# The last V tile in one load, w3 in two loads of two rows per partition, and w3's products by halves, in a one-token attention-and-MLP decode kernel

## The chip, the cores and the metric

The kernel runs on one core of a Trainium2 chip, as one launch. The metric is device time in microseconds (us), from three timed runs of which the median counts. Lower is better. A core has five engines with an instruction queue each: TensorE (PE for products, PEld for the loading of their stationary operand), VectorE (DVE), ScalarE (ACT), GpSimd (POOL) and SyncE (SP), which here only issues transfers. All transfers between memory outside the core and on-chip memory are carried out by 16 DMA engines.

## The reference, cut to what matters

Eight sequences, one new token each (B = 8), model width D = 512. Attention has 32 query heads over 8 key-value heads of width 128 and sees the last 2048 positions of the caches. Then follows an MLP block with two layer norms one after the other; its first part multiplies by w1 and w2 only token-shifted values, which are zero for a single token, so that only w3 (512 x 1792) and w4 (1792 x 512) remain.

```python
def _A_ref(x, k_cache, v_cache, wq, wo):
    ...
    k = jnp.repeat(k_cache[:, :, Sk - W:, :], rep, axis=1)
    v = jnp.repeat(v_cache[:, :, Sk - W:, :], rep, axis=1)
    scores = jnp.einsum("bhqd,bhkd->bhqk", q, k) * (Dh ** -0.5)
    p = _softmax(scores, axis=-1)
    o = jnp.einsum("bhqk,bhkd->bhqd", p, v)
    return (lambda x, *d: x.transpose(*d))(o, 0, 2, 1, 3).reshape(B, Sq, Hq * Dh) @ wo
...
    h2 = _gelu(_layernorm(x1, axis=-1) @ w3) @ w4
    return x1 + h2

x = A_x
h = x + _A_ref(_layernorm(x, axis=-1), A_k_cache, A_v_cache, A_wq, A_wo)
h2 = h + _B_ref(_layernorm(h, axis=-1), B_w1, B_w2, B_w3, B_w4)
```

All inputs and the output are bf16. Some 79 MB are read: 32 MB of K, 32 MB of V, 4 MB each of wq and wo, 1.75 MB each of w3 and w4 (MB of 2^20 bytes).

## The kernel before, in words

The caches come in 16 units n = 0 to 15: a unit is one sequence b = n // 2 and four of its heads. `load_k(n)` (L469) and `load_v(n)` (L475) fetch one unit of K or V as 128 partitions of 16,384 bytes, 2 MB in all, into rings of four buffers, `knat` and `vnat`. V of load 15 is the exception: four loads of 512 KB, 4096 bytes per partition, each with a semaphore of its own (`sem_vl`, L194). SP issues every load of the kernel in one written order, all through the function at L202, one after the other: the K and V units, two loads of wo of 1 MB on the way, then V of load 15, four loads of wo of 512 KB, w3, w4. A load waits on SP for the products that used its buffer last.

Each engine's work is listed by hand in program order (`Engine.op`, L60), with the semaphores that it waits for; each engine runs its list in that order. TensorE's work on a unit is four transposes of K (L308), two groups of scores (L323), and later, with the softmax done, the products of the probabilities with V (`pe_PV`, L406), in four quarters w = 0 to 3 of a unit. For the last three units each quarter is 16 products of 128x128 with 16 columns (`f_last`, L410, L414), whose result DVE scales (L448) and TensorE turns (`turn_o`, L454, L460) and DVE copies to `o2` (L465).

The end of the kernel is this list on TensorE: quarters of V 13 and 14; quarter 0 of V 15, the turn of unit 14, quarters 1 to 3 of V 15; `pe_wo` for the first four groups of wo (L498 to L503; 4 small products that add x at L496, then 64 at L501); the turn of unit 15; `pe_wo` for the last four groups (64 at L501). The result is h transposed: h's 512 columns lie as four column blocks nb of 128 x 8 in `hT_ps`. Then come the two layer norms: column sums by a product with a constant matrix (L627, L648), small DVE steps (L624 to L631, L651 to L654) and two ACT steps (L649, L650). `hb` (L628) is h minus its mean, in bf16, and is what the products with w3 take; the norm's factor comes in later, at L661.

w3 is loaded in four loads of 128 rows of w3 each, 3584 bytes per partition, which share one semaphore (L606, L607). The products with w3 (`pe_w3`, L641) are 14 output blocks f with four products each, one for each block kc of 128 rows: 28 for the first half of the blocks, into one PSUM bank, then 28 for the second half, into another. The stationary operand takes every fourth column of w3, every second for the last two blocks (`w3_cols`, L636). The first of them waits for `hb` and for all four loads. After each half DVE multiplies (L661) and ACT applies GELU (L663). Then TensorE adds the residual (L667) and runs the products with w4 (L676), four at a time in four column strips of the array, in parts that wait for GELU's two halves and for w4's loads: 28 products with w4's first two loads, 4, 16 with the third (`sem_w4b`), 8 with the fourth (`sem_w4c`). DVE and ACT copy the result (L685, L687), and SP stores it (L690).

Of the kernel before, what the change touches and what calls it, by code (L numbers as in the profile page):

```python
# [11 lines left out]
B = 8  # L12
# [10 lines left out]
FC = F // 128  # L23
KC = D // 128
# [6 lines left out]
U = 4  # L31
RR = 32
NCU = W // RR
UL = NCU * DH

NK = 4
NV = 4
# [44 lines left out]
def bass_sequential_preLN__sliding_block_cached__mixer_s_mlp__decode_kernel(  # L82
# [19 lines left out]
    NUN = NB * NU  # L102
# [4 lines left out]
    with es:  # L107
        sb = lambda shape, dtype, name: es.enter_context(nc.sbuf_tensor(name, shape, dtype))
        ps_t = lambda shape, dtype, name: es.enter_context(nc.psum_tensor(name, shape, dtype))
        S = lambda name: es.enter_context(nc.semaphore(name))  # L110

        knat = sb([128, NK, UL], dt.bfloat16, "knat")
        vnat = sb([128, NV, UL], dt.bfloat16, "vnat")
        wbig = sb([128, KC * H * DH], dt.bfloat16, "wbig")
        wq_v = wbig[:, :].rearrange("p (k n) -> p k n", k=KC)
        wo_v = wbig[:, :].rearrange("p (g k n) -> p g k n", g=G, k=R)
        w3_sb = knat[:, 0, 0:KC * F].rearrange("p (k f) -> p k f", k=KC)
        w4_sb = knat[:, 1, 0:FC * D].rearrange("p (c n) -> p c n", c=FC)
# [13 lines left out]
        x_sb = sb([B, D], dt.bfloat16, "x_sb")  # L132
# [33 lines left out]
        at = [0]  # L166

        def tl(n, bf=False):
            t = tail[:, at[0]:at[0] + n]
            at[0] += n  # L170
            return t.bitcast(dt.bfloat16) if bf else t
# [4 lines left out]
        hb = tl(NH // 2, True)  # L176
# [3 lines left out]
        out_sb = sb([B, D], dt.bfloat16, "out_sb")  # L180
# [10 lines left out]

        sem_k = [S(f"sem_k{i}") for i in range(NK)]
        sem_v = [S(f"sem_v{i}") for i in range(NV)]
        sem_vl = [S(f"sem_vl{i}") for i in range(U)]  # L194
        sem_wl = [S(f"sem_wl{i}") for i in range(2)]
        sem_x, sem_wq, sem_wo, sem_w3, sem_w4a, sem_w4b, sem_w4c, sem_out = (
            S(n) for n in ("sem_x", "sem_wq", "sem_wo", "sem_w3", "sem_w4a", "sem_w4b", "sem_w4c", "sem_out"))
        PE, AC, DV, PO, SP = (Engine(S(n)) for n in ("s_pe", "s_act", "s_dve", "s_pool", "s_sp"))

        def dma(eng, dst, src, sem, *waits):  # L200
            def f(e):
                e.dma_start(dst, src).then_inc(sem, 16)  # L202
            eng.op(f, *waits, inc=False)
# [16 lines left out]
        e = DV.op(lambda e: e.bn_stats(st6[:, :], x_sb[:, :]), X)  # L220
        e = DV.op(lambda e: e.bn_aggr(mv[:, :], st6[:, :]), e)
        e = AC.op(lambda e: e.activation(rstd[:, :], mv[:, 1:2], ACT.Sqrt, bias=eps1[0:B, :], scale=1.0), e, e_eps)
        e = DV.op(lambda e: e.reciprocal(rstd[:, :], rstd[:, :]), e)
# [30 lines left out]
        e = PE.op(pe_xT, e_xln, e_idb)  # L254
# [12 lines left out]
        e = DV.op(lambda e: e.tensor_scalar(q_d, S_ps[0][:, 0:H * B], inv_sqrt_dh, None, ALU.mult), e_q)  # L267
# [17 lines left out]
        e_T, e_Tlo, e_Thi, e_lo, e_hi, e_QK, e_PV = {}, [], [], [], [], {}, {}  # L285
# [111 lines left out]
            e_rL[b] = DV.op(lambda e: e.tensor_tensor(rLk[:, s, :, :], r_bc, k_bc, ALU.mult), e_r, e_mK)  # L397

        def V(n, w):
            if n == NUN - 1:  # L400
                return sem_vl[w], 16
            return sem_v[n % NV], 16 * (n // NV + 1)

        e_ev_o, e_fold = {}, {}
# [70 lines left out]
        def load_v(n):  # L475
            b, t = divmod(n, NU)
            src = A_v_cache[b, J * t:J * (t + 1), W0:SK, :].rearrange("j (r c) d -> r j (c d)", r=RR)
            if n < NUN - 1:
                dma(SP, vnat[:, n % NV, :], src, sem_v[n % NV], e_PV.get(U * (n - NV + 1) - 1))
                return  # L480
            for w in range(U):
                cs = slice(w * UL // U, (w + 1) * UL // U)
                dma(SP, vnat[:, n % NV, cs], src[:, :, cs], sem_vl[w], e_PV.get(U * (n - NV + 1) - 1))

        def load_wo(m, sem, g=2):
            dma(SP, wo_v[:, m:m + g, :, :].rearrange("p g k n -> p g (k n)"),
                A_wo[m * R * DH:(m + g) * R * DH, :].rearrange("(g p k) n -> p g (k n)", p=128, k=R), sem, e_q)

        hT_ps = S_ps[0]
        e_wo = []  # L490

        def pe_wo(groups, *waits):
            def f(e):
                if groups[0] == 0:
                    for nb in range(KC):
                        e.matmul(hT_ps[:, nb * B:(nb + 1) * B], x_sb[:, nb * 128:(nb + 1) * 128],  # L496
                                 ident_b[0:B, 0:B], start=(nb == 0), stop=False, skip_group_check=True)
                for g in groups:  # L498
                    for k in range(R):
                        for nb in range(KC):  # L500
                            ins = e.matmul(hT_ps[:, nb * B:(nb + 1) * B], wo_v[:, g, k, nb * 128:(nb + 1) * 128],  # L501
                                           o2[:, g, k, :], start=False, stop=(g == G - 1 and k == R - 1),
                                           skip_group_check=True)  # L503
                return ins
            e_wo.append(PE.op(f, e_exp[NB - 2], X, *waits))
# [32 lines left out]
        for n in range(NUN):  # L538
# [4 lines left out]
            if n >= LVD:  # L543
                load_v(n - LVD)
            if n in WO_AT:
                load_wo(WO_G[WO_AT.index(n)], sem_wo)
            i = U * n
# [35 lines left out]
        for n in range(NUN - LVD, NUN):  # L583
            load_v(n)
# [15 lines left out]
        for a in range(2):  # L600
            for g in (WO_L + 2 * a, WO_L + 2 * a + 1):
                load_wo(g, sem_wl[a], 1)
            pe_wo((WO_L + 2 * a, WO_L + 2 * a + 1), e_scale[NUN - 1], (sem_wl[a], 32))
        e_gl = AC.op(lambda e: e.activation(scratch[:, 1:2], scratch[:, 0:1], ACT.Sqrt), e_warm)

        for k in range(KC):  # L606
            dma(SP, w3_sb[:, k, :], B_w3[128 * k:128 * (k + 1), :], sem_w3, e_T[U * (NUN - NK + 1) - 1])  # L607
        FA = 12
        w4_a = B_w4[0:FA * 128, :].rearrange("(a p c) n -> p a (c n)", p=128, c=4)
        for a, sem in ((0, sem_w4a), (1, sem_w4a), (2, sem_w4b)):  # L610
# [10 lines left out]
        def bc(a, k=KC):  # L621
            return bass.AP(tensor=a.tensor, offset=a.offset, ap=[a.ap[0], [0, k], [1, B]])
# [5 lines left out]
        e_hb = DV.op(lambda e: e.tensor_tensor(v3(hb[:, :]), v3(hs[:, :]), bc(st1), ALU.add), e_mu, e_hs)  # L628
        e = DV.op(lambda e: e.tensor_tensor(v3(hc[:, :]), v3(hs[:, :]), bc(st1), ALU.add))
        e = DV.op(lambda e: e.tensor_tensor(hsq[:, :], hc[:, :], hc[:, :], ALU.mult), e)  # L630
# [3 lines left out]
        FH = FC // 2  # L634

        def w3_cols(kc, f):  # L636
            a, c = divmod(f, 4)
            s = 4 if a < 3 else 2
            return w3_sb[:, kc, 512 * a + c:512 * a + c + 127 * s + 1:s]

        def pe_w3(e, n, f0, f1):  # L641
            for f in range(f0, f1):
                for kc in range(KC):
                    ins = e.matmul(y_ps[n][:, f * B:(f + 1) * B], w3_cols(kc, n * FH + f),
                                   hb[:, kc * B:(kc + 1) * B], start=(kc == 0), stop=(kc == KC - 1))
            return ins

        e = PE.op(lambda e: e.matmul(st2, ones_v[:, :], vsum[:, :], start=True, stop=True), e_vs, e_sc[NUN - 1])  # L648
# [3 lines left out]
        e_r1 = DV.op(lambda e: e.reciprocal(rr[:, B:2 * B], vv[:, B:2 * B]), e1)  # L652
        e = DV.op(lambda e: e.tensor_tensor(v3(xb[:, :]), v3(hc[:, :]), bc(rr[:, B:2 * B]), ALU.mult), e_r1)
        e_fin = DV.op(lambda e: e.tensor_tensor(p32(fin[:, :]), v3(hs[:, :]), v3(xb[:, :]), ALU.add), e, e_pad)  # L654
        e_y = [PE.op(lambda e: pe_w3(e, 0, 0, FH), e_hb, (sem_w3, 16 * KC), e_lo[-1], e_hi[-1], e_lo[-2], e_hi[-2]),
               PE.op(lambda e: pe_w3(e, 1, 0, FH))]
        e_gT = []
        for n in range(2):
            cs = slice(n * FH * B, (n + 1) * FH * B)
            gs = slice(n * FH * 32, (n + 1) * FH * 32)  # L660
            e = DV.op(lambda e, n=n, cs=cs: e.tensor_tensor(v3(g_x[:, cs]), v3(y_ps[n][:, 0:FH * B]),  # L661
                                                            bc(rr[:, 0:B], FH), ALU.mult), e_y[n], e_rr)
# [3 lines left out]
        z_ps = S_ps[1][:, 0:128]  # L666
        PE.op(lambda e: e.matmul(z_ps, fin[:, :], ident_f[:, :], start=True, stop=False, skip_group_check=True),  # L667
              e_fin, e_exp[NB - 1])
        for lo, hi, waits in ((0, FH, (e_gT[0], (sem_w4a, 32))),
                              (FH, 8, (e_gT[1],)),  # L670
                              (8, FA, ((sem_w4b, 16),)),
                              (FA, FC, ((sem_w4c, 16),))):
            def pe_w4(e, lo=lo, hi=hi):
                for fc in range(lo, hi):
                    for nb in range(KC):
                        ins = e.matmul(z_ps[32 * nb:32 * (nb + 1), :], gT[:, fc * 32:(fc + 1) * 32],  # L676
                                       w4_sb[:, fc, nb * 128:(nb + 1) * 128], start=False, stop=(fc == FC - 1),
                                       tile_position=(0, 32 * nb), skip_group_check=True)
                return ins
            e_z = PE.op(pe_w4, *waits)  # L680
        e_out = []
        for nb in range(KC):
            o, z = out_sb[:, nb * 128:(nb + 1) * 128], z_ps[32 * nb:32 * nb + B, :]
            if nb % 2:
                e_out.append(AC.op(lambda e, o=o, z=z: e.activation(o, z, ACT.Copy), e_z))  # L685
            else:
                e_out.append(DV.op(lambda e, o=o, z=z: e.tensor_copy(o, z), e_z))  # L687
# [39 lines left out]
```

## Time and profile before

| What | Value |
|---|---|
| timed runs, median (lowest to highest) | 195.89 us (195.77 to 195.93) |
| the profiled execution's own time | 195.99 us |
| its span, first to last instruction | 194.7 us |
| mean granted TensorE clock | 0.893 of full speed; 0.50 from 170 us to the end |
| PE / PEld / DVE / ACT / POOL busy | 75% / 59% / 51% / 46% / 4% of the span |
| DMA engines busy in slices 2 to 38 of 40 | 90% or more in each |
| read from memory | 79.18 MB, 407 GB/s over the span |
| DMA packets | 7506 |

All times inside the kernel are us from the start of the span. About 1.3 us of the profiled time lie outside the span. A DMA packet is one contiguous run that one DMA engine moves: a load of 128 partitions gives each of the 16 engines 8 of them, and 4-byte ones for the semaphore. A load has landed when the last of the 16 engines is through; the semaphore events in the trace tell when each of them was.

### The profile page before, as it was taken

The page shows a single profiled execution, that of the slowest core. Times are in us where ns is not written, and L with a number is a line of the kernel's source. Part 1 is how long each engine was busy: PE and PEld are TensorE (multiplying, and loading weights), DVE is VectorE, ACT ScalarE, POOL GpSimd, SP SyncE. Part 2 cuts the span into 40 slices and gives each one's busy share as a digit, 9 for nine tenths or more (in the row PEclk, how much of TensorE's full clock was granted, in tenths as well). Part 3 has the DMA queues.
Part 4 walks back from the last instruction along what each step waited for, and adds up shares of the span by engine and source line. Part 5 has one row for each costly group of instructions (what it writes and reads, how often), then busy time and mean ns, then how long its engine had stood idle before and what let it go on. Part 6 is the DMA issues. An engine that isn't in the chain of part 4 may idle for free.

```text
span 194.7 us, 4474 instructions
## 1 busy us (share of the span) xinstructions
PE 146.1 (75%) x1972; PEld 115.0 (59%) x1972; DVE 100.1 (51%) x256; ACT 89.6 (46%) x115; POOL 7.7 (4%) x29
## 2 busy tenths in 40 slices
PE   0028985978999794969498868988497897879765
PEld 0027862765768564746495738765485674768653
DVE  5402445785667582738165664468154975731131
ACT  6000566764848453745153824564264754250041
POOL 5001101001000100010001000010000000000000
PEclk9999999999999999999759997999889999655555
DMA  6999999999999999999999999999999999999981
GB/s 224 431 428 431 428 431 428 428 428 426 424 405 437 431 431 419 431 421 424 428 418 433 424 417 428 431 424 426 431 428 431 431 421 431 411 397 406 410 342 56
DMA packets 7506, 79.46 MB, mean 408 GB/s; under 512 B 816, under 2 KB 832, under 8 KB 3392
## 3 DMA queue, kind: packets, MB, share of 16 engines
q1 hardware_dynamic: 7472, 79.18, 96.7%
q8 instruction: 15, 0.25, 0.5%
q14 instruction: 3, 0.02, 0.0%
q10 hardware_dynamic: 16, 0.01, 0.0%
HBM read 79.18 MB, written 0.01 MB: 407 GB/s over the span
## 4 chain that ended last, share of the span: by engine, by line
DMA 51%; PE 30%; DVE 9%; SPq 6%; ACT 2%; issue 2%
DMA knat<-in_A_k_cache_dram 43%; PE kT_ps L308 18%; DMA knat<-in_B_w_dram 8%; SPq L202 6%; PE S_ps L323 5%; DVE kT_sb L296 5%; PE kT_ps L380 3%; DVE mcol L333 1%; DVE Pz L369 1%; PE sm L442 1%; ACT kT_sb L295 1%; ACT P_sb L354 1%; DVE Mrow L339 1%; PE sm L337 1%; PE S_ps L676 1%
## 5 line engine op out<-in xcount | busy, mean ns | idle before, releaser
L295 ACT ACTIVATE kT_sb<-kT_ps 128x1024 bf16<-128x1024 bf16 x64 | 62.8, 1023 | 44.4 <-PE kT_ps L308 44.4
L308 PE MATMUL kT_ps<-perm_k,knat 128*128 128x128 f32 x512 | 72.0, 299 | 12.1 <-DMA knat<-in_A_k_cache_dram 11.6
L308 PEld LDWEIGHTS kT_ps<-perm_k,knat 128*128 128x128 f32 x512 | 63.5, 154 | 19.9 <-DMA knat<-in_A_k_cache_dram 13.5
L296 DVE TENSOR_SCALAR kT_sb<-kT_ps 128x512 int32<-128x512 int32 x64 | 43.8, 689 | 38.5 <-PE kT_ps L308 38.4
L323 PE MATMUL S_ps<-kT_sb,qz 128*32 128x512 bf16 x256 | 19.9, 384 | 6.6 <-DVE kT_sb L296 3.9
L369 DVE TENSOR_TENSOR Pz<-P_sb,mJ 128x256 bf16<-128x256 bf16 x64 | 23.9, 416 | 0.0
L424 PE MATMUL oT_ps<-vnat,pS 128*32 128x256 bf16 x416 | 17.7, 280 | 0.4 <-DMA vnat<-in_A_v_cache_dram 0.4
L433 ACT ACTIVATE oE<-oT_ps 128x256 f32<-128x256 f32 x13 | 5.0, 384 | 26.6 <-PE oT_ps L424 26.6
L295 ACT ACTIVATE pS<-kT_ps 128x1024 bf16<-128x1024 bf16 x8 | 8.2, 1024 | 10.7 <-PE kT_ps L380 10.7
L323 PEld LDWEIGHTS S_ps<-kT_sb,qz 128*32 128x32 bf16 x256 | 4.6, 94 | 11.5 <-ACT kT_sb L295 10.8
L424 PEld LDWEIGHTS oT_ps<-vnat,pS 128*32 128x32 bf16 x416 | 9.3, 97 | 3.5 <-DMA vnat<-in_A_v_cache_dram 0.5
L296 DVE TENSOR_SCALAR pS<-kT_ps 128x512 int32<-128x512 int32 x8 | 5.5, 692 | 10.4 <-PE kT_ps L380 10.4
L380 PE MATMUL kT_ps<-perm_p,Pz 128*128 128x128 f32 x64 | 9.6, 298 | 0.0
L262 PE MATMUL S_ps<-xlnT,wbig 128*128 128x8 bf16 x128 | 3.6, 168 | 8.0 <-DMA wbig<-in_A_wq_dram 8.0
L280 POOL COPY qz<-q_sb 64x64 bf16<-64x64 bf16 x16 | 4.6, 290 | 119.4 <-PE S_ps L323 103.3
L380 PEld LDWEIGHTS kT_ps<-perm_p,Pz 128*128 128x128 f32 x64 | 7.6, 151 | 3.0 <-issue 3.0
L333 DVE TENSOR_REDUCE mcol<-S_ps 128x1 f32<-128x512 f32 x8 | 5.5, 691 | 5.8 <-PE S_ps L323 5.8
L262 PEld LDWEIGHTS S_ps<-xlnT,wbig 128*128 128x128 bf16 x128 | 3.5, 104 | 8.0 <-issue 8.0
L442 PEld LDWEIGHTS sm<-selo,oE 128*128 128x128 f32 x52 | 7.9, 219 | 0.4 <-ACT oE L433 0.4
L442 PE MATMUL sm<-selo,oE 128*128 128x16 f32 x52 | 7.8, 264 | 0.3 <-DVE negcol L351 0.3
L414 PE MATMUL oT_ps<-pS,vnat 128*128 128x16 bf16 x192 | 6.2, 174 | 1.5 <-DVE oK L448 1.0
L354 ACT ACTIVATE P_sb<-S_ps,negcol 128x512 bf16<-128x512 f32 x8 | 5.5, 687 | 3.8 <-DVE negcol L351 3.8
(91 smaller groups left out, 86.4 us busy)
## 6 DMA issues: line engine op xcount, KB each, us to landing
knat<-in_A_k_cache_dram SPq DMA_DIRECT2D x16, 2048.0 KB, 30.3
vnat<-in_A_v_cache_dram SPq DMA_DIRECT2D x15, 2048.0 KB, 33.5
wbig<-in_A_wq_dram SPq DMA_DIRECT2D x1, 4096.0 KB, 12.5
wbig<-in_A_wo_dram SPq DMA_DIRECT2D x2, 1024.0 KB, 32.9
vnat<-in_A_v_cache_dram SPq DMA_DIRECT2D x4, 512.0 KB, 10.5
wbig<-in_A_wo_dram SPq DMA_DIRECT2D x4, 512.0 KB, 12.2
knat<-in_B_w_dram SPq DMA_DIRECT2D x4, 448.0 KB, 13.3
knat<-in_B_w_dram SPq DMA_DIRECT2D x3, 512.0 KB, 15.1
```

The source lines that it names most:

```text
L202: e.dma_start(dst, src).then_inc(sem, 16)
L262: ins = e.matmul(S_ps[0][:, h * B:(h + 1) * B], wq_v[:, kc, h * DH:(h + 1) * DH], xlnT[:, kc * B:(kc + 1) * B], start=(kc == 0), stop=(kc ...
L295: e_lo.append(AC.op(lambda e: e.activation(dst[:, 0:1024], ps[:, 0:1024], ACT.Copy), e_Tlo[k], *free))
L296: e_hi.append(DV.op(lambda e: e.tensor_single_scalar(dst[:, 1024:2048].bitcast(dt.int32), ps[:, 1024:2048].bitcast(dt.int32), 0, ALU.bitwi ...
L308: ins = e.matmul(ps[:, c * 128:(c + 1) * 128], src[:, c * 128:(c + 1) * 128], perm_k[:, :], is_transpose=True)
L323: ins = e.matmul(S_ps[b % 2][32 * j:32 * (j + 1), :].rearrange("p (c r) -> p c r", c=16), qz[:, b % 2, J * t + j, k, lo:lo + 32], kT[:, j, k],
L333: e_max[b] = DV.op(lambda e: e.tensor_reduce(mcol[:, :], S_ps[b % 2][:, :], AX.X, ALU.max), e_QK[4 * b + 3], e_mT.get(b - 1))
L354: e_exp[b] = AC.op(lambda e: e.activation(P_sb[:, :], S_ps[s][:, :], ACT.Exp, bias=negcol[:, s:s + 1], scale=1.0, accum_out=lcol[:, s:s + 1]),
L369: e_Pz[b, part] = DV.op(lambda e, o=o, p_bc=p_bc, m_bc=m_bc: e.tensor_tensor(Pz[:, 0, J * o:J * (o + 64)].rearrange("p (x j k) -> p x j k" ...
L380: ins = e.matmul(ps[:, c * 128:(c + 1) * 128], src[:, c * 128:(c + 1) * 128], perm_p[:, :], is_transpose=True)
L424: ins = e.matmul(oT_ps[MO * q:MO * (q + 1), NO * (n % 2):NO * (n % 2 + 1)], pS[:, b % 2, o:o + 2 * MO - 1:2], vnat[:, n % NV, (16 * w + 2 ...
L442: ins = e.matmul(sm[:, 32:48], oE[:, o:o + 128], selo[:, 16 * s:16 * s + 16], start=(s == 0), stop=(s == 2 * VP - 1))
```

## The change

V of load 15 becomes one load like the other units', with the unit's semaphore, so that all four quarters of V 15 wait for the whole 2 MB. w3 becomes two loads: load a brings rows 256a to 256a + 255, two neighbouring rows in each partition, 7168 bytes per partition, each with its own semaphore. Row 256a + 2p + k of w3 then lies in partition p, so h's columns are taken in the same order: `hcol(nb)` picks every second of 256 columns, where x, wo and w4 are read and where the output is written. The products with w3 run by halves of w3's rows: for load 0 both halves of the output blocks (14 + 14 products), then for load 1 (14 + 14). The count of products is the same; SP issues 5 loads fewer. The built programs agree in the order of work on all engines but for this.

```diff
         def V(n, w):
-            if n == NUN - 1:
-                return sem_vl[w], 16
             return sem_v[n % NV], 16 * (n // NV + 1)
...
-            if n < NUN - 1:
-                dma(SP, vnat[:, n % NV, :], src, sem_v[n % NV], e_PV.get(U * (n - NV + 1) - 1))
-                return
-            for w in range(U):
-                cs = slice(w * UL // U, (w + 1) * UL // U)
-                dma(SP, vnat[:, n % NV, cs], src[:, :, cs], sem_vl[w], e_PV.get(U * (n - NV + 1) - 1))
+            dma(SP, vnat[:, n % NV, :], src, sem_v[n % NV], e_PV.get(U * (n - NV + 1) - 1))
...
+        def hcol(nb):
+            at = 256 * (nb // 2) + nb % 2
+            return slice(at, at + 255, 2)
...
-                        e.matmul(hT_ps[:, nb * B:(nb + 1) * B], x_sb[:, nb * 128:(nb + 1) * 128],
+                        e.matmul(hT_ps[:, nb * B:(nb + 1) * B], x_sb[:, hcol(nb)],
...
-                            ins = e.matmul(hT_ps[:, nb * B:(nb + 1) * B], wo_v[:, g, k, nb * 128:(nb + 1) * 128],
+                            ins = e.matmul(hT_ps[:, nb * B:(nb + 1) * B], wo_v[:, g, k, hcol(nb)],
...
-        for k in range(KC):
-            dma(SP, w3_sb[:, k, :], B_w3[128 * k:128 * (k + 1), :], sem_w3, e_T[U * (NUN - NK + 1) - 1])
+        for a in range(2):
+            dma(SP, w3_sb[:, 2 * a:2 * a + 2, :].rearrange("p k f -> p (k f)"),
+                B_w3[256 * a:256 * (a + 1), :].rearrange("(p k) f -> p (k f)", k=2), sem_w3[a],
+                e_T[U * (NUN - NK + 1) - 1])
...
-        def pe_w3(e, n, f0, f1):
-            for f in range(f0, f1):
-                for kc in range(KC):
+        def pe_w3(e, n, a):
+            for f in range(FH):
+                for kc in (2 * a, 2 * a + 1):
                     ins = e.matmul(y_ps[n][:, f * B:(f + 1) * B], w3_cols(kc, n * FH + f),
-                                   hb[:, kc * B:(kc + 1) * B], start=(kc == 0), stop=(kc == KC - 1))
+                                   hb[:, kc * B:(kc + 1) * B], start=(kc == 0 and f == 0), stop=(kc == KC - 1),
+                                   skip_group_check=True)
...
-        e_y = [PE.op(lambda e: pe_w3(e, 0, 0, FH), e_hb, (sem_w3, 16 * KC), e_lo[-1], e_hi[-1], e_lo[-2], e_hi[-2]),
-               PE.op(lambda e: pe_w3(e, 1, 0, FH))]
+        for a in range(2):
+            e_y = [PE.op(lambda e, n=n, a=a: pe_w3(e, n, a), e_hb, (sem_w3[a], 16), e_lo[-1], e_hi[-1], e_lo[-2],
+                         e_hi[-2]) for n in range(2)]
...
-                                       w4_sb[:, fc, nb * 128:(nb + 1) * 128], start=False, stop=(fc == FC - 1),
+                                       w4_sb[:, fc, hcol(nb)], start=False, stop=(fc == FC - 1),
...
-            o, z = out_sb[:, nb * 128:(nb + 1) * 128], z_ps[32 * nb:32 * nb + B, :]
+            o, z = out_sb[:, hcol(nb)], z_ps[32 * nb:32 * nb + B, :]
```

More of the change, by code (lines that the diff above doesn't have):

```diff
@@ L193, in bass_sequential_preLN__sliding_block_cached__mixer_s_mlp__decode_kernel @@
         sem_v = [S(f"sem_v{i}") for i in range(NV)]
-        sem_vl = [S(f"sem_vl{i}") for i in range(U)]
         sem_wl = [S(f"sem_wl{i}") for i in range(2)]
-        sem_x, sem_wq, sem_wo, sem_w3, sem_w4a, sem_w4b, sem_w4c, sem_out = (
-            S(n) for n in ("sem_x", "sem_wq", "sem_wo", "sem_w3", "sem_w4a", "sem_w4b", "sem_w4c", "sem_out"))
+        sem_w3 = [S(f"sem_w3{i}") for i in range(2)]
+        sem_x, sem_wq, sem_wo, sem_w4a, sem_w4b, sem_w4c, sem_out = (
+            S(n) for n in ("sem_x", "sem_wq", "sem_wo", "sem_w4a", "sem_w4b", "sem_w4c", "sem_out"))
         PE, AC, DV, PO, SP = (Engine(S(n)) for n in ("s_pe", "s_act", "s_dve", "s_pool", "s_sp"))
```

## The prediction, made before the changed kernel ran

> **What bounds the kernel now.** First the page's slices: the DMA engines are busy nine tenths or more from the second slice to the thirty-eighth, and the tail is where that ends.
>
> ```profile
> PE   0028985978999794969498868988497897879765
> ...
> PEclk9999999999999999999759997999889999655555
> DMA  6999999999999999999999999999999999999981
> GB/s 224 431 428 431 428 431 428 428 428 426 424 405 437 431 431 419 431 421 424 428 418 433 424 417 428 431 424 426 431 428 431 431 421 431 411 397 406 410 342 56
> ```
>
> The reader sees a stream that never pauses, at about 430 GB/s while K and V come in 16,384-byte packets, and at about 405 in the last slices, in which V 15, wo, w3 and w4 come in packets of 4096 and 3584 bytes. Second, the chain that ended last, from 175 us on (start, length, what):
>
> ```profile
> 176.33 15.20 DMA knat<-in_B_w_dram
> 191.53 0.04 issue
> 191.57 0.62 PE S_ps L676 x16
> 192.19 0.01 issue
> 192.20 0.44 PE S_ps L676 x6
> ```
>
> The third w4 load lands at 191.53 and releases 16 products. The fourth was issued at 176.8 with 15.3 us to landing; the semaphore events put its last engine at 192.16, and 0.04 us later the last 8 products begin. So the last landing sets the end. Third, the end of the timeline and the windows, for the room on TensorE:
>
> ```profile
> 177.22 0.51 PEld L414 LDWEIGHTS oT_ps<-pS,vnat 128*128 128x128 bf16 x16 [0.50 <-issue]
> ...
> 179.46 0.47 PEld L501 LDWEIGHTS S_ps<-o,wbig 128*128 128x128 bf16 x15
> 180.74 0.35 PEld L501 LDWEIGHTS S_ps<-o,wbig 128*128 128x128 bf16 x10 [0.81 <-issue]
> ```
> ```profile
> 187.84 1.88 PEld L644 LDWEIGHTS kT_ps<-Pz,knat 128*128 128x128 bf16 x56 [1.06 <-DMA knat<-in_B_w_dram]
> ...
> 189.64 0.50 PEld L667 LDWEIGHTS S_ps<-ident_f,Pz 128*128 128x128 f32 x2
> ...
> 190.37 0.81 PEld L676 LDWEIGHTS S_ps<-knat,Pz 128*32 128x32 bf16 x32 [0.23 <-ACT Pz L663]
> 191.57 0.35 PEld L676 LDWEIGHTS S_ps<-knat,Pz 128*32 128x32 bf16 x16 [0.39 <-DMA knat<-in_B_w_dram]
> ```
>
> TensorE waits 1.06 us for w3, is then busy to 191.2, and waits 0.39 for w4's third load. w4's products take 0.10 us per round of four (32 in 0.81), so the last 8 could begin 12 rounds or 1.22 us after the first, at 190.40 + 1.22 = 191.62. They begin at 192.20: TensorE has 0.58 us to spare before its own chain would set the end.
>
> **The change part by part.** *The stream, V 15.* Its bytes stay, its packets go from 512 of 4096 bytes to 128 of 16,384. By the semaphore events the last engine was through with V 13 at 168.18, with V 14 at 173.11 and with the four pieces of V 15 at 174.39, 175.66, 176.95 and 178.23: 5.12 us for the pieces, 4.90 and 4.93 for the two units before. So -0.22 us, and V 15 lands at 178.01. The windows give the other end:
>
> ```profile
> DMA packets 529, 7.73 MB, mean 430 GB/s; under 512 B 57, under 2 KB 57, under 8 KB 57
> ```
> ```profile
> DMA packets 808, 3.02 MB, mean 408 GB/s; under 512 B 89, under 2 KB 89, under 8 KB 802
> ```
>
> The first is 150 to 168 us, the second 171 to 178.4; 2.10 MB take 4.88 us at 430 GB/s and 5.14 at 408, so -0.26.
>
> *The stream, w3.* 512 packets of 3584 bytes become 256 of 7168, of which the trace has none. The last engine needed 187.79 - 183.32 = 4.47 us for its 32, 0.140 each; a packet of 16,384 costs 4.90/8 = 0.613. The straight line through both gives 0.272 for 7168, 16 of them 4.35: -0.12. By the windows' rates, with the time per byte a constant plus a share per packet, 7168 bytes would run at 420 GB/s against 404: 1.84 MB, -0.16. The lower end is 0, if the longer packets cost as much per byte as the short ones.
>
> Sum of the stream: -0.22 - 0.12 = -0.34 by the last engine, -0.42 by the mean rates, -0.22 without w3's share. I take **-0.35**, near the last engine's, since it is the last engine that the end waits for. wo and w4 keep their packets and their order, so every later landing moves up by this: w3's second half to 187.45, w4's first two to 189.93, the fourth to 191.82. The Trainium skill, page "DMA: Bandwidth & Descriptors", section "Anatomy of one DMA — SWDGE (gpsimd) path", gives a load a fixed cost of about 2.0 us, for another issuing path; five loads fewer would then be an estimated 10 us. The four pieces landed 1.28 us apart, of which their bytes at 430 GB/s are 1.22, so the trace leaves 0.06 us per load and disagrees for loads queued behind one another.
>
> *SP's queue.* It loses three issues of about 0.60 us (L202, V) and two w3 issues of over 1 us. It ends its issuing at 179.8 while the first engine finishes w4's third load at 187.77, so the cover is 8 us and this is worth nothing.
>
> *The wait for all of V 15.* Quarter 0 began at 177.22, held by DVE's L448; now it waits for 178.01 + 0.04 = 178.05: +0.8 us. Behind it on TensorE stand the turn of unit 14, the other quarters, both parts of `pe_wo`, the turn of unit 15 and the two norm products; DVE and ACT wait for these. The norm's second product was at 186.28 to 186.87; +0.8 is 187.08 to 187.67. At the other end the pause of 0.91 us between weight loads at 179.83 and 180.74, which no wait of the program explains, would be a fetch of instructions (the page's queue q8; its packet at 178.36 took 1.09 us) that runs under the wait: then the delay is 0.1 at least. I take +0.8.
>
> *w3's products.* Before, 56 began at 187.84. Now the first 28 need only w3's first load, and begin when the norm's second product is off the array, at about 187.57 (186.52 for its last pass, + 0.8, + 0.25 for the pass). All 56 at 0.0335 (1.88/56) end at 189.41 instead of 189.66, and the second load, at 187.45, has long landed when the 29th comes at 188.5. So what the halves save is 0.25 us: the wait for w3 is replaced by the wait for V 15. Without the halves the w3 products could have begun no earlier, since the norm is late; what they would buy with an early norm, about 1 us, is not there. `hb`, the factors and L654 come 0.8 later too, 188.9 at the latest, and the residual product needs them at 189.41. w4's products begin at 190.15, after the w4 loads' 189.97. Their last 8 could begin at 190.15 + 1.22 = 191.37; the landing lets them at 191.86. TensorE's room is 0.49 us: the landing still ends last.
>
> *Columns in steps of two.* Stationary operand of x and wo: the windows at L644 count 48 products with step four in 1.61 us (0.0335 each) and the last 8, with step two, in 0.21 (0.026), as fast as L501's 0.027 with step one: nothing. Moving operand of w4: the scores (L323) read K in steps of two, 8 products of 512 columns in 0.62 us, two rounds of four; by the ratio to 128 columns in 0.107 at clock 0.50, a round of 512 at the full clock is 0.21, and twice that would not fit: nothing. The output's copies write 128 elements with a step, 0.28 us now; DVE's L465 writes with a step of eight and takes 0.22 for 16 elements, less than these: 0, at most +0.1 if each step cost a little.
>
> *Sum:* 195.99 - 0.35 = 195.64 for the profiled execution; it lay 0.10 above the median of 195.89, so **195.54** against that.
>
> **The rivals.** *TensorE ends last, and the gain is lost.* Where: V 15's wait carries on, and a pause like that at 180.0 comes again in w3's products, behind the next fetch (q8 packet at 184.47, later by 0.8). For it: that pause follows a fetch, and as the page's 15 fetches serve 3944 TensorE instructions, 263 each, the next boundary comes some 130 products on, within w3's first ten. Against: that fetch was over at 185.55, and TensorE needed nothing until 187.84. Price: w4 begins at 190.15 + 0.9 = 191.05, the last 8 at 192.27 against 192.20: +0.07. It decides from a pause of 0.49 on. The Trainium skill, "Runtime: NRT & Kernel Launch", section "Instruction fetch mechanics", calls such crossings mostly hidden, which speaks against it; the pause at 180.0 speaks for it.
>
> *Steps of two slow the moving side of w4, and the kernel is slower.* If each round took twice 0.107, the first 12 from 190.15 would end at 192.7 and the last 2 at 193.1, where they ended at 192.4: +0.7, 196.6. It costs something where a round takes over 0.14 (0.10 + 0.49/12), and turns the sign over 0.17 (2.05 us from 190.15 to 192.20, over 12). The scores' row speaks against it.
>
> *The change does not do what it says:* the longer loads go out in the same small packets. Then 195.9. Against it: the 15 other V loads are in 16,384-byte packets in the window above. *A fixed cost per load comes off besides:* the events leave 0.06 us per load, 0.30 for five, if none of it is the packets' own: 195.2. By the figure of the page named above it would be some 186, which no row bears out.
>
> **How the numbers follow.** A measurement of this kernel can tell about 0.2%, or 0.39 us, from no change. The forecast's case, a gain of 0.22 to 0.45, has 0.70, half of it beyond 0.39; TensorE last, -0.1 to +0.5, 0.15, of which 0.05 over +0.39; steps of two 0.07; no longer packets 0.05; fixed cost 0.03. Faster 0.35 + 0.03 = 0.38, slower 0.05 + 0.07 = 0.12, same 0.50. The forecast's own range is 195.35 to 195.7. The range over the cases reaches from 195.2, a little beyond the mean rates' end, to 196.05, into the lost gain, and leaves out the last rows of each side.
>
> **What would show it.** Right: V 15 about 4.9 us behind V 14 on the last engine; w3's loads 2.2 us apart; TensorE held by V 15 near 178.05; 28 w3 products from about 187.6; the last 8 of w4 still begun by the landing, near 191.86. Wrong: a pause within w3's products, w4's last part begun without a DMA wait, rounds of four over 0.11 us, or w3's landing no earlier than 187.8.

## The result, and the profile after

The changed kernel takes 195.53 us (median of 22 runs, 195.37 to 195.97) against 195.81 of the kernel before in the same series (22 runs, 195.58 to 196.36): 0.9985 of it, 95% interval 0.9978 to 0.9991, that is 0.28 us less (0.18 to 0.43). A second series with 11 runs gave 0.9981 (0.9973 to 0.9990). The forecast was 0.35 less. The profiled execution has a span of 194.2 us against 194.7; of these 0.5 us only a part is the change, as the landings below show. The timed 195.53 lies 0.01 from the forecast's 195.54, inside its 195.35 to 195.7; the kernel before was itself 0.08 faster in this series than in the earlier one, so the gain, 0.28 for 0.35, is the fairer comparison.

The page's slices and its count of packets:

```profile
DMA  6999999999999999999999999999999999999981
GB/s 218 432 432 432 429 432 432 429 432 424 429 394 440 425 430 419 429 425 429 429 423 424 425 429 429 422 425 427 422 422 425 429 429 432 425 419 402 417 349 56
DMA packets 6787, 79.46 MB, mean 409 GB/s; under 512 B 737, under 2 KB 753, under 8 KB 2545
```

The reader sees the same unbroken stream, and 719 packets fewer: 384 of V 15, 256 of w3 and 80 of semaphores make 720. The thirty-sixth slice, which holds most of V 15's transfers, runs at 419 GB/s where it ran at 397.

The chain that ended last, from its last long piece (start, length, what):

```profile
172.82 18.11 DMA knat<-in_B_w_dram
190.93 0.04 issue
190.97 0.62 PE S_ps L677 x16
191.59 0.02 issue
191.61 0.43 PE S_ps L677 x8
```

As before, w4's third load (landed 190.93) releases 16 products and its fourth (191.56 by the semaphore events) the last 8, 0.05 us later. The timeline shows what TensorE's weight loads waited for on the way:

```profile
177.69 0.50 PEld L412 LDWEIGHTS oT_ps<-pS,vnat 128*128 128x128 bf16 x16 [1.40 <-DMA vnat<-in_A_v_cache_dram]
...
179.93 0.47 PEld L498 LDWEIGHTS S_ps<-o,wbig 128*128 128x128 bf16 x15
180.66 1.38 PEld L498 LDWEIGHTS S_ps<-o,wbig 128*128 128x128 bf16 x49 [0.26 <-issue]
...
186.43 2.07 PEld L643 LDWEIGHTS kT_ps<-Pz,knat 128*128 128x128 bf16 x56
...
188.42 0.50 PEld L668 LDWEIGHTS S_ps<-ident_f,Pz 128*128 128x128 f32 x2
...
189.80 0.81 PEld L677 LDWEIGHTS S_ps<-knat,Pz 128*32 128x32 bf16 x32 [0.88 <-ACT Pz L664]
190.97 0.35 PEld L677 LDWEIGHTS S_ps<-knat,Pz 128*32 128x32 bf16 x16 [0.36 <-DMA knat<-in_B_w_dram]
```

TensorE is now held by V 15 at 177.69. The pause without a named cause after the first 15 wo products is still there, but its end is at 180.66, where it was at 180.74: V 15's wait ran inside it. w3's 56 products begin right behind the norm, at 186.64, 1.2 us earlier than before (the row at 186.43 is their first weight load, which still overlaps the norm's product), and all three parts of w4 wait for their landings. (The row at 189.80 names ACT; GELU was done at 189.13, and w4's first two loads landed at 189.70.)

The stretches of the last engine's stream, from the semaphore events of each profile (last of the 16 increments of a load, us):

| Kernel | V 14 landed | V 15 | wo | w3 | w4 | V 15 + w3 |
|---|---|---|---|---|---|---|
| before | 173.11 | 5.12 | 5.09 | 4.47 | 4.37 | 9.59 |
| before, second profile | 172.78 | 5.12 | 5.43 | 4.51 | 4.39 | 9.63 |
| changed | 172.75 | 4.90 | 5.15 | 4.39 | 4.37 | 9.29 |
| changed, second profile | 172.83 | 4.90 | 5.30 | 4.39 | 4.38 | 9.29 |
| V 15 alone | 172.79 | 4.90 | 5.08 | 4.58 | 4.40 | 9.48 |
| w3 alone | 172.57 | 5.12 | 5.23 | 4.35 | 4.40 | 9.47 |
| old product order | 172.84 | 4.97 | 5.07 | 4.38 | 4.33 | 9.35 |
| w3 in one load | 172.61 | 4.97 | 5.04 | 4.35 | 4.38 | 9.32 |

The two loads that were changed went from 9.61 to 9.29 us. V 14's landing, which the change can't touch, scatters over 0.5 us, and wo, which it left alone, over 0.4. So one profile's span says nothing at this size; the stretches of the changed loads do. They aren't free of chance either: V 14, one load in every kernel, took 4.93 us behind V 13 in the first profile of before and 5.09 in the second, where a fetch of instructions in between made another engine the last (the section on the hardware has these steps).

### The profile page after: what moved, and what is told of

Its sections match the earlier page's. It is cut to its first block, busy times and chain, and to the rows that moved or that the text cites. A ratio compares the mean times of both kernels' runs of the same rounds, so it can differ in the third digit from the quotient of the medians.

```text
span 194.2 us, 4469 instructions
## 1 busy us (share of the span) xinstructions
PE 142.3 (73%) x1972; PEld 111.1 (57%) x1972; DVE 99.8 (51%) x256; ACT 89.5 (46%) x115; POOL 7.8 (4%) x29
## 4 chain that ended last, share of the span: by engine, by line
DMA 70%; PE 14%; DVE 8%; SPq 5%; ACT 1%; issue 1%
DMA knat<-in_A_k_cache_dram 60%; PE kT_ps L308 10%; DMA knat<-in_B_w_dram 9%; SPq L202 5%; DVE kT_sb L296 4%; PE S_ps L323 3%; DVE Pz L369 2%; DVE mcol L333 1%; PE S_ps L677 1%; PE kT_ps L380 1%; ACT kT_sb L295 0%; ACT P_sb L354 0%; ACT out_sb L686 0%; DVE Mrow L339 0%; PE sm L337 0%
## 5 line engine op out<-in xcount | busy, mean ns | idle before, releaser
L308 PE MATMUL kT_ps<-perm_k,knat 128*128 128x128 f32 x512 | 67.6, 288 | 14.5 <-DMA knat<-in_A_k_cache_dram 14.2
L308 PEld LDWEIGHTS kT_ps<-perm_k,knat 128*128 128x128 f32 x512 | 59.9, 148 | 22.1 <-DMA knat<-in_A_k_cache_dram 16.2
L412 PEld LDWEIGHTS oT_ps<-pS,vnat 128*128 128x128 bf16 x192 | 5.8, 105 | 3.6 <-DMA vnat<-in_A_v_cache_dram 3.0
```

The costliest lines, as they stand in the source:

```text
L308: ins = e.matmul(ps[:, c * 128:(c + 1) * 128], src[:, c * 128:(c + 1) * 128], perm_k[:, :], is_transpose=True)
L412: ins = e.matmul(oT_ps[:, 0:16], vnat[:, n % NV, (16 * w + c) * DH:(16 * w + c + 1) * DH], pS[:, b % 2, o:o + 31:2], start=(w == 0 and c = ...
```

## The experiments

Theory A: the last engine's landings set the end, and the change shortens its stream by sending longer packets. Its rivals were B, that the gain comes from TensorE's products with w3; C, that the whole 0.5 us of the two spans is the change; D, that a load costs something by itself, so that fewer loads are the gain; E, that the stream isn't what sets the pace. F and G are about why one engine is last.

**The changed kernel again, and the kernel before again.**

> The changed kernel once more, as the reference of this call. Theory A (the last DMA engine's landings set the end, and the change shortens its stream): 0.2 to 0.35 us under the kernel before, w4's last load lands about 18.8 us after V 14 on the last engine. Theory B (the gain comes from TensorE's chain after w3): the same time, but w4's last part begins later than 0.05 us after its landing. Theory C (most of the profile's 0.5 us of span is the change): 0.5 us under the kernel before.

Measured: 195.53 us, 0.9981 (0.9973 to 0.9990) of the kernel before; V 14 to w4's last landing 18.97 us, 0.16 over the expected 18.8, as wo took 0.15 longer than in the first profile; the last products begun 0.04 us behind it.

> The kernel before once more, for a second profile. Nothing in the change lies ahead of V 15, so V 14's landing on the last engine (173.11 us in the first profile, 172.6 to 172.9 in the five changed ones) should differ by chance only: with it the span, 194.3 to 194.7. From V 14 on the sum of 19.05 us to w4's last landing should come again within 0.1, as should the pause in wo's products, which ends at 180.7.

Measured: 195.82 us, no change; V 14 at 172.78, but wo 5.43 and the sum 19.45, so the sum did not come again within 0.1. The pause ended at 180.05, not 180.7: it follows its fetch, whose packet came 0.71 us earlier here. C falls: V 14's 0.36 us between the first two profiles is chance.

**V 15 alone.** The kernel before with the V part of the diff and nothing else:

```diff
...
-            if n < NUN - 1:
-                dma(SP, vnat[:, n % NV, :], src, sem_v[n % NV], e_PV.get(U * (n - NV + 1) - 1))
-                return
-            for w in range(U):
...
+            dma(SP, vnat[:, n % NV, :], src, sem_v[n % NV], e_PV.get(U * (n - NV + 1) - 1))
```

> The kernel before with V of load 15 in one load and nothing else. Theory A: V 15 lands 4.90 us after V 14 on the last engine, w3 takes 4.47 us behind wo, w4's last load comes 18.85 to 18.95 after V 14 (19.05 in the kernel before): 0.15 to 0.2 us under the kernel before. TensorE's wait for V 15 is swallowed by the pause in wo's products, which shrinks from 0.91 us to about 0.4. Theory B: no faster than the kernel before, or slower by up to 0.5 us, since TensorE waits for V 15 and the 56 products with w3 still come in one piece.

Measured: 195.59 us, 0.9987 (0.9978 to 0.9996), 0.25 us less, a little more than expected. V 15 took 4.90 us. The timeline of its TensorE products:

```profile
177.74 0.60 PE L411 MATMUL oT_ps<-pS,vnat 128*128 128x16 bf16 x16 [0.90 <-DMA vnat<-in_A_v_cache_dram]
...
179.98 0.56 PE L493 MATMUL S_ps<-o,wbig 128*128 128x8 bf16 x15
180.73 1.47 PE L493 MATMUL S_ps<-o,wbig 128*128 128x8 bf16 x49 [0.19 <-issue]
```

Held by V 15 and yet through the pause when the kernel before was: the wait costs nothing, and the kernel is faster without any halves. This speaks against B.

**w3 alone.** The changed kernel with V of load 15 in four loads and four semaphores again (the removed lines of `V` and `load_v` put back).

> The changed kernel with V of load 15 in four loads again: only w3's part of the change is left. Theory A: V 15 takes 5.12 us behind V 14, w3 4.39 behind wo, w4's last load comes 18.95 to 19.0 after V 14: 0.05 to 0.12 us under the kernel before. The pause in wo's products is back at 0.9 us. Theory B: all of the gain, 0.28 us, or more, since TensorE is also free of the wait for V 15.

Measured: 195.67 us, 0.9993 (0.9984 to 1.0002), 0.14 us less, which the interval does not tell from nothing; w3 took 4.35 us. V 14 to w4's last landing took 19.10 us, not the expected 18.95 to 19.0, since wo took 5.23. That w3's part is a gain is thus shown by its stretch and not by the time. Together the two parts make 0.39, the whole 0.28 and 0.37. The timeline of its TensorE products:

```profile
178.85 0.56 PE L506 MATMUL S_ps<-o,wbig 128*128 128x8 bf16 x15
180.74 1.47 PE L506 MATMUL S_ps<-o,wbig 128*128 128x8 bf16 x49 [1.32 <-issue]
```

TensorE came to the pause 0.6 us earlier than in the kernel before, and left it at the same 180.74.

**The products in the old order.** The changed kernel, all 56 products waiting for both w3 loads:

```diff
...
-        for a in range(2):
-            e_y = [PE.op(lambda e, n=n, a=a: pe_w3(e, n, a), e_hb, (sem_w3[a], 16), e_lo[-1], e_hi[-1], e_lo[-2],
-                         e_hi[-2]) for n in range(2)]
+        e_y = [PE.op(lambda e, n=n: pe_w3(e, n), e_hb, (sem_w3[0], 16), (sem_w3[1], 16), e_lo[-1], e_hi[-1], e_lo[-2],
+                     e_hi[-2]) for n in range(2)]
```

> The changed kernel with w3's 56 products in the old order, all waiting for both loads. Theory A: within 0.05 us of the changed kernel; the products begin at about 187.2, 0.5 us later, and w4's first part at or shortly after its landing near 189.8, so that its last part still waits for the fourth load. Theory B: the gain of 0.28 us is lost, back to the time of the kernel before.

Measured: 195.42 us, 0.9977 (0.9968 to 0.9986), 0.1 us under the changed kernel of the same series, which the intervals do not tell from none. Its products:

```profile
187.39 2.04 PE L643 MATMUL kT_ps<-Pz,knat 128*128 128x8 bf16 x56 [0.65 <-DMA knat<-in_B_w_dram]
189.30 0.77 PE L667 MATMUL S_ps<-ident_f,Pz 128*128 128x128 f32 x2
190.00 2.04 PE L676 MATMUL S_ps<-knat,Pz 128*32 128x128 bf16 x56
```

w3's products begin 0.75 us later than in the changed kernel, w4's 0.17, and the end comes no later. B falls: the halves buy nothing here.

**Packets or loads.** The price was scaled up to all 16 V units, with the products waiting for whole units as before: first four loads of 4096 bytes per partition, then four of 16,384 bytes on 32 partitions.

```diff
...
-            dma(SP, vnat[:, n % NV, :], src, sem_v[n % NV], e_PV.get(U * (n - NV + 1) - 1))
+            for w in range(U):
+                cs = slice(w * UL // U, (w + 1) * UL // U)
+                dma(SP, vnat[:, n % NV, cs], src[:, :, cs], sem_v[n % NV], e_PV.get(U * (n - NV + 1) - 1))
```

> The changed kernel with every V unit in four loads of 4096 bytes per partition on the unit's own semaphore; the products wait for all four as before. Theory A, packet length: 4096-byte packets cost the last engine 0.22 us per unit of 2 MB, 16 units 3.5 us; between 2.8 and 4.5 us slower than the changed kernel, and 5.1 us per V unit in the stream in place of 4.9. Theory D, a cost per load: the same here, and the next kernel tells them apart. Theory E (the stream is not what sets the pace in the middle of the kernel): under 1 us slower.

Measured: 198.98 us, 1.0155 (1.0141 to 1.0169) of the kernel before, so 3.1 us over it and 3.4 over the changed kernel: 0.21 us per unit, where V 15 by itself showed 0.22. The last four V units landed 5.12 us apart on the last engine, as expected.

```diff
...
+            for w in range(U):
+                dma(SP, vnat[32 * w:32 * (w + 1), n % NV, :], src[8 * w:8 * (w + 1)], sem_v[n % NV],
+                    e_PV.get(U * (n - NV + 1) - 1))
```

> The changed kernel with every V unit in four loads of 32 partitions each, 16,384 bytes per partition: as many loads as the kernel with 4096-byte pieces, packets as long as in the changed kernel. Theory A, packet length: within 0.6 us of the changed kernel (48 semaphore packets more per engine at 0.009 us are 0.43). Theory D, a cost per load (0.06 us for each of 48 loads more, 2.9 us, or more): 2.5 us slower at least.

Measured: 310.04 us. Both theories missed, for a reason that lies in neither: each of these loads raised its semaphore in 9 steps and not in 16, one at the issue and 8 as the data landed, so that 8 engines carried V. In many of the page's slices the DMA engines are half busy, at 214 to 219 GB/s. The outer dimension of each load in memory is 8. Half speed for 16 units would add some 78 us (an estimate, 16 times 4.9); the run took 114 longer, and where the rest comes from was not followed. The run tells nothing of A or D. The next one cuts V by heads, 32 partitions in steps of four, with an outer dimension of 32:

```diff
...
+            for w in range(U):
+                dma(SP, vnat[w::J, n % NV, :], src[:, w, :], sem_v[n % NV], e_PV.get(U * (n - NV + 1) - 1))
```

> The changed kernel with every V unit in four loads of one head each: 32 partitions in steps of four, 16,384 bytes per partition, on all 16 DMA engines (the four loads of 32 neighbouring partitions had an outer dimension of 8 and ran on 8). Theory A, packet length: within 0.6 us of the changed kernel (0.43 for the semaphore packets). Theory D, a cost per load: 2.5 us slower or more, as the kernel with 4096-byte pieces, which was 3.4 us slower.

Measured: 195.55 us, 0.9986 (0.9976 to 0.9995): the changed kernel's time with 48 loads more. The windows from 100 to 150 us, in which K and V come, of the kernel with 4096-byte pieces, of this one and of the changed kernel:

```profile
DMA packets 3372, 20.97 MB, mean 419 GB/s; under 512 B 359, under 2 KB 359, under 8 KB 2669
```
```profile
DMA packets 1757, 21.39 MB, mean 428 GB/s; under 512 B 359, under 2 KB 359, under 8 KB 482
```
```profile
DMA packets 1561, 21.41 MB, mean 428 GB/s; under 512 B 166, under 2 KB 166, under 8 KB 283
```

The first two have the same 359 semaphore packets, that is the same loads, and only the first is slow. A holds, and D falls for loads of 512 KB; E had fallen with the 3.4 us of the first.

**How much room TensorE has.** The changed kernel in the old product order, with w3 in one load of four rows per partition:

```diff
...
-            at = 256 * (nb // 2) + nb % 2
-            return slice(at, at + 255, 2)
+            return slice(nb, nb + 509, 4)
...
+        dma(SP, w3_sb[:, :, :].rearrange("p k f -> p (k f)"),
+            B_w3.rearrange("(p k) f -> p (k f)", k=4), sem_w3[0], e_T[U * (NUN - NK + 1) - 1])
```

> The changed kernel with w3 in one load of four rows per partition, 14,336 bytes; h's columns in steps of four; the 56 products wait for the one load. Theory A: w3 takes 4.30 us behind wo in place of 4.39, so w4's last load comes 0.09 earlier; stationary loads of x, wo with step four cost 0.0335 in place of 0.0267 us each, 0.9 us on TensorE's chain for 132 products, which the room before w4's landings covers: 0.0 to 0.1 us under the changed kernel. Rival: the room is smaller than that and TensorE ends last: 0.1 to 0.5 us slower than the changed kernel. If w4's moving side suffers from step four, its rounds of four take over 0.11 us and the end comes later by 0.1 per round.

Measured: 195.86 us, 0.9995 (0.9986 to 1.0003), 0.2 to 0.3 us over the changed kernel by the two ratios, though the intervals overlap. That is in the rival's range, but the rival's reason is the smaller part of it. Its timeline:

```profile
183.05 2.21 PEld L497 LDWEIGHTS S_ps<-o,wbig 128*128 128x128 bf16 x64 [0.43 <-DVE o L463]
...
190.04 1.54 PEld L673 LDWEIGHTS S_ps<-knat,Pz 128*32 128x32 bf16 x56 [0.22 <-ACT Pz L660]
...
191.93 0.91 ACT L682 ACTIVATE out_sb<-S_ps 8x128 bf16<-8x128 f32 x2 [1.92 <-PE S_ps L673]
```

With step four 64 weight loads take 2.21 us instead of 1.78, and w4's 56 weight loads run through in one piece with no wait for a landing. TensorE begins the last 8 products at 191.43, 0.08 us behind the last landing at 191.35 where the changed kernel was 0.05 behind, and the output's copies begin 0.58 us behind that landing where they began 0.50: TensorE has just used up its room and costs under 0.1. The larger part is the output. Its two copies on ACT take 0.91 us where the changed kernel's take 0.64 and those before 0.56, a term that neither side had. From the last landing to the end of the span it is 2.94 us here, 2.60 in the changed kernel and 2.51 before. w4's rounds did not slow (56 in 1.54), and w3 took 4.35 us, not 4.30: one load gained next to nothing over two.

**Which engines are last.** The changed kernel with w4's fourth load cut up:

```diff
...
+        for q in range(16):
+            dma(SP, w4_sb[8 * q:8 * q + 8, FA:FC, :].rearrange("p c n -> p (c n)"),
+                B_w4[FA * 128 + 16 * q:FA * 128 + 16 * q + 16, :].rearrange("(p c) n -> p (c n)", c=FC - FA), sem_w4c)
```

> The changed kernel with w4's fourth load (256 KB) cut into 16 loads of 8 partitions. If a load of 8 partitions runs on 8 of the 16 DMA engines only, always the same ones, those get 0.63 us more of the last bytes and the others none. If they are the engines that lag (fetches of instructions seem to hit the same eight in turn, 1.5 us each time): slower by 0.4 to 0.7 us. If they are the eight that are through first, at 188.2: faster by about 0.5 us. If the loads spread over all 16: within 0.2 us.

Measured: 197.97 us, 1.0095 (1.0071 to 1.0119), some 2.2 us over the changed kernel by the ratios. The 16 loads raised their semaphore 144 times, 9 each: 8 engines. The last landing came 2.59 us behind the third load's in place of 0.63:

```profile
194.61 0.14 PEld L678 LDWEIGHTS S_ps<-knat,Pz 128*32 128x32 bf16 x8 [2.24 <-DMA knat<-in_B_w_dram]
```

The direction is that of lagging engines that get the bytes. The size is not: the extra 1.96 us is three times the 0.64 of 8 packets more. A cost of 0.16 us for each of the 16 loads would fit it, so that the smallest loads may have a cost of their own, but no run separates it. In this profile w4's first two loads, which come before the 16, landed 0.63 us later behind w3 than in the changed kernel too, and that stays unexplained. The run shows less cleanly than meant which engines lag.

**More TensorE instructions.** The changed kernel with 128, then 280 products more that nobody reads, while TensorE waits for wq:

```diff
+        def pe_extra(e):
+            for _ in range(280):
+                ins = e.matmul(S_ps[1][:, 0:B], ident_b[:, :], ident_b[:, 0:B], start=True, stop=True)
+            return ins
+        PE.op(pe_extra)
```

> The changed kernel with 128 small products more on TensorE while it waits for wq (they are read by nobody). Theory F: a fetch of 256 TensorE instructions delays one of eight DMA engines by 1.5 us, each in turn, so that the first and the ninth fetch make the engine that ends last; one fetch more, the sixteenth, hits an engine that has had one: within 0.2 us of the changed kernel. Rival G: the last engine's lag has another cause: also no change. The next kernel tells them apart.

Measured: 195.64 us, 0.9993 (0.9984 to 1.0003), 0.2 us over the changed kernel by the ratios, whose intervals overlap; no change, as both expected.

> The changed kernel with 280 small products more on TensorE while it waits for wq. Theory F: two fetches more, the seventeenth hits the engine of the first and the ninth a third time; if that is before its last bytes, the last landing comes up to 1.5 us later: 0.5 to 1.6 us slower than the changed kernel. Rival G: within 0.2 us of it.

Measured: 197.02 us, 1.0055 (1.0037 to 1.0073), 1.4 us over the changed kernel by the ratios. The size is F's, the cause is not. The profiled run is the slowest of the four (196.67 to 198.03), and in it the seventeenth fetch came at 191.08, when the engine it would hit was nearly through, and w4's last load landed at 191.87. What came late is TensorE:

```profile
181.41 0.18 PEld L418 LDWEIGHTS oT_ps<-pS,vnat 128*128 128x128 bf16 x4 [1.40 <-issue]
...
187.69 0.42 PEld L504 LDWEIGHTS S_ps<-o,wbig 128*128 128x128 bf16 x13 [2.10 <-issue]
...
192.88 1.42 PEld L683 LDWEIGHTS S_ps<-knat,Pz 128*32 128x32 bf16 x56 [0.23 <-ACT Pz L670]
```

Two pauses of 1.40 and 2.10 us, each ended 1.45 to 1.48 us after a fetch's packet, push w4 to 192.88 and make TensorE the last in this run: the forecast's rival, brought about by moving the fetch boundaries.

## Why the prediction was right, point by point

*What bounds the end: right.* In the changed kernel the last 8 products begin 0.05 us behind the last landing, and neither the V wait nor the order of w3's products makes the time longer.

*V 15's term, -0.22: right*, 5.12 to 4.90 in both pairs of profiles, 4.90 to 4.97 in the other kernels of the table with one load, and 0.21 per unit over 16. *w3's term, -0.12: right*, 4.49 to 4.39 in the pairs; over all profiles, four loads take 4.47 to 4.58 and two 4.35 to 4.41. The packets of 7168 bytes, which the trace of before did not have, took 0.275 us each where the line gave 0.272. Sum of the two stretches -0.32, forecast -0.34. (The mean rates' share for w3 comes to -0.17 by the prediction's own 420 and 404 GB/s, not -0.16; the forecast did not go by it.)

*The rest up to the timed -0.28* is inside its interval. One term was put at nothing and has a size: the output's copies in steps of two, 0.31 us each on ACT where they took 0.27, two in a row. The row before, then the one after:

```profile
192.66 0.56 ACT L685 ACTIVATE out_sb<-S_ps 8x128 bf16<-8x128 f32 x2 [2.32 <-PE S_ps L676]
```
```profile
192.06 0.64 ACT L686 ACTIVATE out_sb<-S_ps 8x128 bf16<-8x128 f32 x2 [2.94 <-PE S_ps L677]
```

From the last landing to the end of the span the kernel before takes 2.51 and 2.52 us in its two profiles, the changed one 2.60 and 2.58. These 0.07 are within the +0.1 that the prediction allowed. -0.32 + 0.07 = -0.25.

*The wait for V 15, +0.8 carried on: wrong in size, and the other end of its range was right.* TensorE began quarter 0 at 177.70 (0.45 later, V 14 having landed 0.36 earlier in this profile), and left the pause 0.08 earlier than before. The pause goes with the fetch of instructions: in ten pauses of nine profiles it ended 1.25 to 1.52 us after the end of a q8 packet, whenever TensorE had come to it (179.06 to 180.39 in the eight that have it behind the 15th wo product). The old-order kernel and the one with 128 products more, held by V 15 until 177.85 and 177.83, came there at 180.47 and 180.45, and 0.11 and 0.07 us over the usual spacing of the weight loads are left of the pause, which ends 1.45 us after the packet in both. The step was hidden: with TensorE's room 0.1 or 0.8 gives the same end, so the time tests the stream's terms and not this one.

*w3's products, "what the halves save is 0.25 us": the reason was wrong.* The norm was not late, since the wait for V 15 was not carried on; the products began at 186.64, not 187.57, and were over 1.2 us earlier than before; then w4's weight loads waited 0.88 us. It still buys nothing, for the reason given first, the landings.

*The columns in steps of two: right* for weight loads (64 in 1.78 us before and after) and for w4's rounds (32 in 0.81 in both); step four cost 0.43 us per 64 weight loads. For the output's copies it was not quite nothing, as said.

*The fixed cost of a load: right to leave it out.* 48 loads of 512 KB more changed nothing. The Trainium skill's 2.0 us per load (page "DMA: Bandwidth & Descriptors", section "Anatomy of one DMA — SWDGE (gpsimd) path", for another issuing path) does not appear for these loads, queued behind one another. For 16 loads with one packet per engine some 0.16 us each would fit.

*The rival "TensorE ends last"* did not happen in the changed kernel. It did in one neighbour, with the fetch boundaries moved, and by less than 0.1 us in another, with step four. The Trainium skill's "Runtime: NRT & Kernel Launch", section "Instruction fetch mechanics", says that crossing a block is mostly hidden; here it is so only because the stream ends later still, and the pauses of 0.1 to 2.1 us say that the fetch itself is not hidden.

## What to carry to other kernels

When a kernel ends on a full stream of transfers, price an edit by packets: their count and length on the engine that ends last, read from differences of landings. Those of V 15 and w3 came again within some 0.1 us, where the time of one run scatters by 0.6; that of wo did not, so take a stretch from several profiles. How many loads the bytes come in counted for nothing here, as long as each had 512 KB, used all 16 engines and was queued in time; the length of each contiguous run counted 0.2 us per 2 MB between 4 and 16 KB. A layout that is free where data is read can cost where the output is written: look at the instructions behind the last landing, whose 0.07 us were added to the end in full here. A wait added on an engine with room costs nothing until it uses up that room, so find the next pause behind it before carrying it to the end.

## What the runs showed of the hardware that was not expected

The engine that ends last lags the first by 3.4 us (V 14's landings in the changed kernel: 169.31 for the first, 172.75 for the last). The lag comes in steps. The trace does not name the engine of a landing, but the 16 landings of each load can be followed from one load to the next. Wherever one fetch of 16,384 bytes of TensorE instructions (queue q8, 15 in the kernel) lies alone between two loads of K or V, 105 times in 11 profiles, exactly one of the 16 landings has moved back by 1.46 to 1.79 us against the others, 1.54 in the middle, and the other 15 have kept their places within 0.1 us.

The fetches seem to hit the same eight engines in turn. In the changed kernel the first three put one engine each at 1.55, 1.65 and 1.90 us behind the first engine; the ninth to eleventh move those that then stand at 1.52, 1.62 and 1.93 to 3.08, 3.15 and 3.45. The engine that lands V 14 last has fallen back twice, but it is not the same one in all profiles: in the kernel before's first it fell behind the first and the ninth fetch (to 2.33, then from 2.28 to 3.79), in the changed kernel's first behind the third and the eleventh (at 157.30, between the landings at 152.87 and 162.96), in its second again behind the first and the ninth. So theory F's premise, that the first and the ninth make the last engine, does not hold for every run. The thirteenth fetch comes while wo is loaded, and this is why wo scatters: where it makes a further engine the last, wo's stretch is 5.15 to 5.43 us in the table, and otherwise 5.04 to 5.09. With 280 products more the ninth comes at 96.11, and the step, from 2.10 to 3.71, lies between the landings at 95.71 and 101.80: the step moves with the fetch. That the loads of 8 partitions ended late fits these eight. An experiment that takes the fetches away was not made, so what they cost the kernel as a whole stays open.

The loads of this case whose slowest dimension in memory is 8, on 32 partitions and on 8, ran on 8 of the 16 engines: 9 steps of their semaphore. With 32 there all 16 were used.
